# Mamba2 scan and PReLU layer: the order of the third and fourth weight piece, w_out's scales and the rows' scan

## The chip, the cores and the metric

One core of one Trainium2 chip runs the whole program. The time is in microseconds of the device, the median of the runs; less is better. In what follows PE is TensorE (matmuls), DVE is VectorE, ACT is ScalarE, POOL is GpSimd and SP is SyncE, which here only issues DMAs. Each engine works through its own list of instructions in order and waits at an instruction whose inputs aren't there.

## The reference

Two stages in a row: a scan over the sequence in chunks with decays (4 sequences, 8 heads, 768 steps, head size 32, state size 16), and a layer with PReLU on its 3072 x 256 result.

```python
log_a = np.log(np.clip(a, 1e-06, 1.0))
for c in range(nc):
    cum = np.cumsum(la, axis=-1)
    L = np.exp(cum[:, :, :, None] - cum[:, :, None, :]) * causal
    CB = np.einsum('bhin,bhjn->bhij', Cc, Bc)
    y_intra = np.einsum('bhij,bhjd->bhid', CB * L, xc)
    y_inter = np.einsum('bhin,bhnd->bhid', Cc, state) * np.exp(cum)[:, :, :, None]
    y[:, :, sl] = y_intra + y_inter
    state = decay_full[:, :, None, None] * state + np.sum(Bx, axis=2)

x = y.transpose(0, 2, 1, 3).reshape(3072, 256)
h = x @ w_in                                    # 256 -> 2048
g = np.maximum(h, 0.0) + alpha * np.minimum(h, 0.0)
out = g @ w_out                                 # 2048 -> 256
```

The inputs x, a, B, C and alpha are float32; w_in and w_out arrive as float64.

## The kernel before

**Tiling.** The kernel takes chunks of 128 steps, two chunks to a pair, so 12 pairs (pair 0 to 11). Four chunks make a group of 512 tokens. The hidden width of 2048 is cut into 16 blocks f of 128. Group 0 goes block by block: hidden(0, f) is one block's product with w_in and its PReLU (ACT scales by s_alpha, DVE takes the maximum with s_mul times the product), and output(f) the product with w_out, four blocks behind. The groups after it go four blocks at a time (quad and product), with fewer products from sums of the operands. The order on every engine is the order of the program's text, written by hand (manual_schedule).

**The start.** first_two runs pairs 0 and 1, before any group is whole, and mixes their work with the first weights. For pair 1, on PE: the product of B and C (gram_of), one half of hidden_two(0, 2, 0), then x_products (L942) and state_products (L954). times (L900, DVE) makes the operands of x_products; mask (L929, POOL) those of state_products, four of them, of which the fourth is first read by pair 2. copy_out (L962 and L963, four copies on ACT) takes the result out of PSUM into xT; only then can PE multiply the second half of the tokens: hidden_two(0, 0, 2Q, bank(3)), and after first_two, from L1471 on, hidden_two(0, 2, 2Q). hidden_two returns prelu_of[...]: called with False it issues the scaling on ACT alone (L1149), called without it the DVE part (L1154) too, and the scaling where that hasn't been issued.

**Weight pieces.** Both weights are loaded in pieces of 512 KB of float64 (load_next, load_weights, L274), which SP issues, into six buffers "raw". The list pieces holds w_in's first two pieces, and then w_in and w_out by turns: piece 2, the third, is w_in for blocks f = 4 and 5, and piece 3 w_out's first, for f = 0 and 1. A piece is made into float32 from its 32-bit halves in six steps:

- ACT: the absolute of the high half, into wt (L290)
- POOL: a clamp of wt, in place (L295)
- DVE: the sign bit of the high half, into wr (sign, L318)
- DVE: a shift of wt and its xor with wr, into wr (convert_b, L330)
- ACT: the low half, into wg (low; L301 for w_in, for w_out L304 twice, with scales g_mul and g_add by block)
- POOL: wr + wg as whole numbers, into the weight (convert, called by convert_next, L352)

convert_a issues the first two and low; with later=True it returns low, for the caller to issue. g_mul and g_add come from slope_signs (L415): s_mul, of 128 x 16, times 2^-11 and times 2^25.

**Loads of pair 2.** load_pair(2, False, True) issues C in four DMAs (L150), B of its first chunk (L218) and x of its first chunk (L223). The second chunk follows as load_bc2() and load_x(1). rows_sent stores what DVE's scan rows_products (L457) made; pieces 4 to 7 and the decays' rows come behind. All of it is in SP's queue, in this order.

**The rows' scan.** rows_scan(0) (a memset, L481, and a scan, L483, on DVE) makes decays of all rows. PE transposes them (rows_turn, L519) in front of hidden(0, 4), ACT copies that (L524), and POOL's L546 multiplies pair 2's B with them.

**After first_two**: L1471 to L1480 (hidden_two, piece 3's convert_next, rows_turn, piece 4's convert_a and convert_next, the loads of pair 2), and then the loop over f from 4: hidden(0, f), a stage of pair 2 (its first instructions on PE are the transposes L684), then output(f - 4) (L1168), which for f = 4 and 5 reads piece 3.

Of the kernel before, what the change touches and what calls it, by code (L numbers as in the profile page):

```python
# [12 lines left out]
ALU = mybir.AluOpType  # L13
ACTF = mybir.ActivationFunctionType
# [8 lines left out]
def kernel(  # L23
# [25 lines left out]
    nc = tc.nc  # L49
# [46 lines left out]
    gp = ctx.enter_context(tc.tile_pool(name="gp", bufs=16))  # L96
# [6 lines left out]
    def bank(i):  # L103


        return ps_q.tile([P, 512], F32, name="bank", tag=f"q{i}")
# [15 lines left out]
    def load_rows(i, eng=nc.sync):  # L122

        rows = ld.tile([RW, Q], F32, name="rows")
        eng.dma_start(out=rows, in_=a.rearrange("b h (c t) -> (b h c) t", t=Q)[i * RW : (i + 1) * RW])
        loads["r", i] = rows
# [5 lines left out]
    def load_heads(i, eng=nc.sync):  # L132

        eng.dma_start(out=heads_a[i].rearrange("(h n) t -> h n t", n=N)[:, 0],
                          in_=a[0, :, 2 * i * Q : 2 * (i + 1) * Q])
# [26 lines left out]
    def load_tokens(dst, src, t0):  # L162


        d = dst.rearrange("p j (h w) -> p j h w", h=H)
        for k in range(2):
            for j in range(2):
                t = t0 + k * Q + j * HQ
                nc.sync.dma_start(out=d[HQ * k : HQ * (k + 1), j],
                                  in_=src[:, t : t + HQ, :].rearrange("h p w -> p h w"))  # L170
# [16 lines left out]
    def load_products(gp, ap):  # L187
        b, c = divmod(2 * gp, CPB)
        rows = scratch["pf", b // 2].rearrange("(b h c) t -> b h (c t)", b=2, h=H)
        rows = rows[b % 2, :, c * Q : (c + 2) * Q]  # L190
        nc.sync.dma_start(out=ap, in_=rows.unsqueeze(1).to_broadcast([H, N, 2 * Q]))

    def load_pair(gp, decays=True, parted=False):


        b, c = divmod(2 * gp, CPB)
        turned = gp > GC
        nat = ldx.tile([P, 3, 2, H * N], F32, name="nat")
        xt = ldx.tile([P, 2, HD], F32, name="xt")

        ap = ldx.tile([P, 2 * Q], F32, name="ap") if gp >= NB else None
        if gp == 0:
            load_rows(0, nc.scalar)
            load_heads(0, nc.scalar)
        elif gp > NB:
            load_products(gp, ap)
        abc = []
        if gp >= HALF:
            load_tokens(nat[:, 0], B[b], c * Q)
        def load_bc(k):  # L210
            ts = slice((c + k) * Q, (c + k + 1) * Q)
            eng = nc.scalar if gp == 0 else nc.sync
            if gp == 0 and k == 0:
                load_groups(nat, 1, C, b, c)
            if gp in (1, 2) and k == 0:
                load_groups(nat, 1, C, b, c)
            for i, src in enumerate((B,) if turned or gp <= NB else (B, C)):
                eng.dma_start(out=nat[:, i, k].rearrange("p (h n) -> p h n", h=H),  # L218
                              in_=src[b, :, ts, :].rearrange("h p n -> p h n"))

        def load_x(k):
            ts = slice((c + k) * Q, (c + k + 1) * Q)
            nc.sync.dma_start(out=xt[:, k].rearrange("p (h d) -> p h d", h=H),  # L223
                              in_=x[b, :, ts, :].rearrange("h p d -> p h d"))

        for k in range((1 if parted else 2) if gp < HALF else 0):
            load_bc(k)
            if gp >= NB:
                load_x(k)
        for k in range(2 if gp < NB and gp else 0):  # L230
            load_x(k)
        for i, src in enumerate((B, C) if turned else ()):
            load_blocks(nat, i, src, b, c)
        for k in range(2 if gp >= NB else 0):
            abc.append(lda.tile([P, H * Q], F32, name="abc"))
        loads["p", gp] = nat, abc, xt, ap
        if gp >= HALF:
            load_tokens(xt, x[b], c * Q)
        if decays:
            for part in load_spread(gp, b, c):  # L240
                pass
        return lambda: load_bc(1), load_x
# [36 lines left out]
    def convert_a(dst, src, sg, by=nc.gpsimd, later=False):  # L279

        if src.dtype == F32:
            return lambda: None
        raw = raws.pop(id(dst))
        hi = raw[:, :, :, 1]
        half = raw.rearrange("p k w t -> p k (w t)").bitcast(U16)
        half = half.rearrange("p k (w t) -> p k w t", t=4)[:, :, :, 1]
        t = wtp.tile([P, 2, WQ], U32, name="wt")
        g = wtp.tile([P, 2, WQ], F32, name="wg")

        nc.scalar.activation(out=t.bitcast(F32), in_=hi.bitcast(F32), func=ACTF.Abs, scale=0.125)  # L290

        parts[id(dst)] = hi, t, g
        if by is nc.vector:
            sign(dst, src, sg)
        by.tensor_scalar(out=t.bitcast(F32), in0=t.bitcast(F32), scalar1=F64_INF,  # L295
                         scalar2=F64_ZERO, op0=ALU.min, op1=ALU.max)


        def low():
            if sg is None:  # L300
                nc.scalar.activation(out=g, in_=half, func=ACTF.Copy, scale=2.0**-11, bias=2.0**25)  # L301
            for i in range(2 if sg is not None else 0):
                f = slice(sg + i, sg + i + 1)
                nc.scalar.activation(out=g[:, i], in_=half[:, i], func=ACTF.Identity,  # L304
                                     scale=g_mul[:, f], bias=g_add[:, f])

        if later:
            return low
        low()
# [61 lines left out]
    for v in range(2):  # L371
        vs = slice(HQ * v, HQ * (v + 1))
        nc.vector.tensor_copy(out=ident_q[vs].rearrange("p (c t) -> p c t", c=4),
                              in_=ident[vs, vs].unsqueeze(1).to_broadcast([HQ, 4, HQ]))
# [21 lines left out]
    s_mul = const.tile([P, NF], F32, name="s_mul")  # L396
# [12 lines left out]
    def slope_signs():  # L409
        if moe_w_out.dtype == F32:  # L410
            nc.vector.tensor_single_scalar(out=s_out, in_=s_mul.bitcast(U32), scalar=SIGN,
                                           op=ALU.bitwise_and)
        else:
            for o, by in ((g_mul, 2.0**-11), (g_add, 2.0**25)):
                nc.gpsimd.tensor_scalar(out=o, in0=s_mul, scalar1=by, scalar2=None, op0=ALU.mult)  # L415


    xts = {}
# [5 lines left out]
    held = {}  # L424
# [36 lines left out]
    def rows_sent(rpf):  # L461
        scratch["pf", 0] = dr.tile([RW, Q], F32, name="pf0")
        nc.sync.dma_start(out=scratch["pf", 0], in_=rpf)
# [14 lines left out]
    def rows_scan(i):  # L478

        d0 = held[i]  # L480
        nc.vector.memset(d0[:, Q : Q + 1], 0.0)  # L481
        pr = prep.tile([RW, Q], F32, name="pr")
        nc.vector.tensor_tensor_scan(out=pr[:, ::-1], data0=d0[:, 1 : Q + 1][:, ::-1],  # L483
                                     data1=ends[:RW, ::-1], initial=0.0,
                                     op0=ALU.mult, op1=ALU.add)
        return pr
# [350 lines left out]
    def first_two():  # L837
# [141 lines left out]
        def one_at_a_time(i, cs):  # L979
            for c in cs:  # L980
                mask(i, slice(c, c + 1))
# [16 lines left out]
                       in_=ident[:RW, : H * CPB].rearrange("p (h c) -> p c h", c=CPB)[:, :4]  # L998
# [23 lines left out]
        low = convert_a(*pieces[0], later=True)  # L1022
# [13 lines left out]
        low = convert_a(*pieces[1], later=True)  # L1036
# [23 lines left out]
        prelu_of = {0: hidden_two(0, 0, 0, first)}  # L1060
# [12 lines left out]
        hidden_two(0, 2, 0, second, (0,))  # L1073
        states(1, dps, pf1, range(3))
        one_at_a_time(1, range(3))
        slope_signs()
        prelu_of[0](False)
        for r in range(4):
            times(1, r, sp[r])
        states(1, dps, pf1, (3,))  # L1080
        mask(1, slice(3, 4))
        rpf = rows_products()
        load_next()
        load_bc2, load_x = load_pair(2, False, True)
        rows_sent(rpf)
        load_next()
        load_bc2()
# [10 lines left out]
        copy_out(1, y)  # L1098
        prelu_of[2] = hidden_two(0, 2, 0, second, (1,))
        prelu_of[0]()  # L1100
        convert_a(*pieces[2])
        sign(*pieces[2])
        prelu_of[2](False)
        convert_b(*pieces[2])
        convert_next(first=False)
        low = convert_a(*pieces[3], later=True)
        prelu_of[1] = hidden_two(0, 0, 2 * Q, bank(3))
        low()
        prelu_of[2]()
        held["pr"] = rows_scan(0)  # L1110
        convert_b(*pieces[3])
        prelu_of[1]()
        state[0] = new[1][:, 3]
# [325 lines left out]
    pieces = in_pieces[:2]  # L1439
# [4 lines left out]
    def load_next(n=1):  # L1444
        for p in pieces[loaded[0] : loaded[0] + n]:
            load_weights(*p)
        loaded[0] += n

    def convert_next(first=True, ready=False, **kw):


        i = done[0]
        if i < len(pieces):
            if not ready:
                convert(*pieces[i], **kw)
            if first and i and i + 2 < len(pieces):
                convert_a(*pieces[i + 2])
            if loaded[0] == i + 6:
                load_next()
        done[0] += 1  # L1460
# [151 lines left out]
```

## Time and profile before

| What | Value |
|---|---|
| median of 3 runs | 357.13 us (356.59 to 357.65) |
| profiled execution | 356.75 us |
| its span, first to last instruction | 355.0 us |
| clock granted to PE | 1.00 throughout |
| data moved by DMA | 29.82 MB |
| DMA share, 22.4 to 40.6 us | 1.00 |

How it is read: the profile tells of one execution on the chip. Busy is time in which an engine executed; PEld is PE's weight loads, which overlap its matmuls. A wait is idle time in front of an instruction, put down to what ended it; "issue" is idle time that nothing in the profile ended. The chain of waits is followed back from the last instruction, at each step to what released it. The DMA share is the mean busy share of 16 DMA engines, and may be over 100% in short windows, since transfers overlap. On a queue's line in the DMA view stand its name, its packets, its MB and its share of the engines' time in the window.

The start in a few rows of the timelines before (us from the span's start):

| Start | Took | Engine | What |
|---|---|---|---|
| 13.15 | 0.67 | SP | issue of piece 2 |
| 14.37 | 0.43 | SP | issue of piece 3 |
| 14.85 | 1.95 | SP | issue of C of pair 2, four DMAs |
| 16.84 | 0.43 | SP | issue of B of pair 2's first chunk |
| 18.27 | 0.84 | ACT | prelu_of[0](False), L1149 twice |
| 20.02 | 0.58 | POOL | g_mul, L415 |
| 20.57 | 0.25 | POOL | g_add, L415 |
| 20.79 | 0.45 | POOL | fourth mask of pair 1, L929 |
| 21.85 | 0.27 | ACT | first copy of pair 1, L962 |
| 22.55 | 0.69 | ACT | piece 2's L290 |
| 28.30 | 0.38 | PE | transposes of pair 2, L684 |

### The profile page before, as it was taken

To read this page: it belongs to the slowest core of one execution; us is meant where nothing else is said; L and a number is where in the kernel's file an instruction comes from. 1 tells how busy PE (TensorE), PEld (TensorE's weight loads), DVE (VectorE), ACT (ScalarE), POOL (GpSimd) and SP (SyncE) were. 2 spreads that over 40 slices of the span, in tenths; PEclk is the share of its full clock that TensorE was granted. 3 is DMA by queue.
4 is the path that set the end of the run, shared out by engine and by line. 5 is a ranking of instruction groups with operands and counts; after the bars stand their busy time and mean duration, and the time that the engine had idled before them with its cause. 6 is when DMAs were issued, how large, how long until landed. Compare 5 with 4: busy or idle time off the path is not lost.

```text
span 355.0 us, 7785 instructions
## 1 busy us (share of the span) xinstructions
PE 347.8 (98%) x2983; PEld 284.2 (80%) x2983; DVE 237.4 (67%) x482; ACT 172.6 (49%) x391; POOL 205.8 (58%) x230
## 2 busy tenths in 40 slices
PE   8989999999999999999999999999999999999996
PEld 4665665678788788888888888888888888888885
DVE  7968986998758756857747847757856633643363
ACT  4468475526256346346345445345445344443431
POOL 7866668589839755725645725647526535434510
PEclk9999999999999999999999999999999999999999
DMA  6889999117245403403413423422001001001102
GB/s 127 211 172 357 240 313 198 59 30 171 92 88 118 98 3 79 101 2 83 81 48 76 83 52 75 83 53 68 9 2 31 0 2 30 2 1 33 30 0 59
DMA packets 99813, 29.82 MB, mean 84 GB/s; under 512 B 73824, under 2 KB 95680, under 8 KB 99776
## 3 DMA queue, kind: packets, MB, share of 16 engines
q1 hardware_dynamic: 97296, 29.00, 34.8%
q10 hardware_dynamic: 2480, 0.32, 0.6%
q8 instruction: 23, 0.38, 0.4%
q14 instruction: 14, 0.11, 0.1%
HBM read 25.94 MB, written 3.37 MB: 83 GB/s over the span
## 4 chain that ended last, share of the span: by engine, by line
PE 92%; DVE 2%; SPq 2%; POOL 1%; DMA 1%; issue 1%; ACT 0%; POOLq 0%; DVEq 0%
PE bank L1242 33%; PE hp L1267 29%; PE bank L1168 8%; PE ss L1267 6%; PE hp L1125 5%; PE ss L803 1%; PE ss L747 1%; PE bank L1235 1%; PE ss L821 1%; PE ss L795 1%; DMA nat<-in_C_dram 1%; PE ss L758 1%; SPq L1466 1%; DVE dec L884 1%; DVE wr L330 1%
## 5 line engine op out<-in xcount | busy, mean ns | idle before, releaser
L1324 POOL TENSOR_TENSOR gt<-gt 128x512 f32<-128x512 f32 x58 | 74.1, 1278 | 21.1 <-DVE gt L1252 16.3
L1242 PE MATMUL bank<-gt,w_out 128*128 128x256 f32 x320 | 83.5, 381 | 0.0
L1242 PEld LDWEIGHTS bank<-gt,w_out 128*128 128x128 f32 x320 | 60.1, 190 | 9.2 <-issue 1.0
L1314 POOL TENSOR_TENSOR gt<-gt 128x512 f32<-128x512 f32 x20 | 25.4, 1270 | 62.6 <-DVE gt L1252 49.0
L1252 DVE SCALAR_TENSOR_TENSOR gt<-hp,s_mul,gt 128x256 f32<-128x256 f32 x96 | 42.0, 479 | 29.1 <-ACT gt L1250 26.9
L1250 ACT ACTIVATE gt<-hp,s_alpha 128x256 f32<-128x256 f32 x96 | 40.3, 472 | 34.5 <-PE hp L1267 31.4
L1242 PE MATMUL bank<-gt,ws 128*128 128x256 f32 x224 | 55.9, 379 | 0.0
L1242 PEld LDWEIGHTS bank<-gt,ws 128*128 128x128 f32 x224 | 42.3, 190 | 5.6
L1267 PE MATMUL hp<-xs,w_in 128*128 128x256 f32 x160 | 41.9, 384 | 0.0
L1267 PE MATMUL hp<-xs,ws 128*128 128x256 f32 x160 | 41.1, 380 | 0.0
L1293 DVE TENSOR_TENSOR hp<-hp,u 128x512 f32<-128x512 f32 x20 | 14.0, 700 | 35.2 <-ACT u L1291 35.2
L1267 PEld LDWEIGHTS hp<-xs,ws 128*128 128x128 f32 x160 | 30.3, 190 | 4.3 <-POOL xs L1209 0.2
L1267 PEld LDWEIGHTS hp<-xs,w_in 128*128 128x128 f32 x160 | 29.7, 190 | 4.5
L1168 PE MATMUL bank<-w_out,gt 128*128 128x256 f32 x128 | 31.2, 386 | 0.7 <-POOL w_out L352 0.7
L1168 PEld LDWEIGHTS bank<-w_out,gt 128*128 128x128 f32 x128 | 23.6, 190 | 7.6 <-issue 3.1
L1267 PE MATMUL ss<-xT,w_in 128*128 128x256 f32 x96 | 24.6, 379 | 0.0
L659 POOL TENSOR_TENSOR sm<-state,bmask 128x256 f32<-128x256 f32 (+1 forms) x10 | 6.2, 618 | 28.9 <-DVE state L656 28.9
L1125 PE MATMUL hp<-xT,w_in 128*128 128x512 f32 x48 | 22.7, 595 | 0.0
L575 DVE TENSOR_TENSOR_SCAN dec<-abc,bank 128x192 f32<-128x192 f32 x48 | 22.7, 522 | 0.0
L1282 ACT COPY m<-hp 128x512 f32<-128x512 f32 x8 | 4.7, 587 | 35.7 <-PE hp L1267 35.7
L1291 ACT COPY u<-hp 128x512 f32<-128x512 f32 x20 | 11.7, 586 | 19.4 <-PE hp L1267 19.4
L1252 DVE SCALAR_TENSOR_TENSOR gt<-c,s_mul,gt 128x256 f32<-128x256 f32 x40 | 20.6, 554 | 0.0
(231 smaller groups left out, 610.4 us busy)
## 6 DMA issues: line engine op xcount, KB each, us to landing
abc<-z SPq DMA_DIRECT2D x24, 192.0 KB
raw<-in_moe_w_in_dram SPq DMA_DIRECT2D x8, 512.0 KB
raw<-in_moe_w_out_dram SPq DMA_DIRECT2D x8, 512.0 KB
abc<-z SPq DMA_DIRECT2D x8, 512.0 KB
out_dram<-o_sb SPq DMA_DIRECT2D x32, 64.0 KB
xt<-in_x_dram SPq DMA_DIRECT2D x12, 128.0 KB
nat<-in_B_dram SPq DMA_DIRECT2D x24, 64.0 KB
xt<-in_x_dram SPq DMA_DIRECT2D x24, 64.0 KB
```

What stands on the lines that cost most here:

```text
L575: nc.vector.tensor_tensor_scan(out=dv[:, o : o + SQ], data0=abc[k][:, s : s + SQ], data1=ident_p[0][:, :SQ], initial=0.0, op0=ALU.mult, op ...
L659: nc.gpsimd.tensor_tensor(out=sm[:, :nk].rearrange("p k (g m) -> p k g m", g=2), in0=new[:, :nk].unsqueeze(2).to_broadcast([P, nk, 2, 2 * D]),
L1125: nc.tensor.matmul(hp, w_in[:, k, f * P : (f + 1) * P], xts[g][:, k], start=(k == 0), stop=(k == KC - 1))
L1168: nc.tensor.matmul(pos[0][t // 2][:, t % 2], gt[:, t * Q : (t + 1) * Q], w_out[:, f], start=(f == 0 and t % 2 == 0), stop=(f == NF - 1), s ...
L1242: nc.tensor.matmul(ms[g][i][:, h], w, blocks[g, z][n][:, p], start=(q == 0 and h == 0), stop=(q == NQ - 1), skip_group_check=True)
L1250: nc.scalar.mul(o[:, p], h[:, p], s_alpha[:, fs[p]])
L1252: nc.vector.scalar_tensor_tensor(out=o[:, p], in0=h[:, p], scalar=s_mul[:, fs[p]], in1=o[:, p], op0=ALU.mult, op1=ALU.max)
L1267: nc.tensor.matmul(to[:, p], w(2 * z + p), b, start=start and p == 0, stop=True, skip_group_check=True)
L1291: nc.scalar.copy(out=u2, in_=A)
L1293: nc.vector.tensor_tensor(out=Y, in0=Y, in1=u2, op=ALU.add)
L1314: nc.gpsimd.tensor_tensor(out=tc_, in0=g22, in1=g12, op=ALU.subtract)
L1324: eng.tensor_tensor(out=o, in0=x0, in1=x1, op=ALU.subtract)
```

## The change

Four edits, all but one in first_two:

- Piece 2's L290 and L295 are issued right behind prelu_of[0](False) and slope_signs, ahead of times, of pair 1's fourth mask and of its copies; its low stays behind prelu_of[0](). prelu_of[0](False) now stands before slope_signs. prelu_of[2](False) moves behind piece 2's convert_b and convert_next.
- slope_signs makes g_mul and g_add on ACT instead of POOL.
- rows_scan(0) is issued before prelu_of[2](False), and so before the DVE part of prelu_of[2] and piece 3's sign and xor; before, it stood behind prelu_of[2]().
- load_pair gets an argument between, called after each load_bc in its loop. With load_next there, piece 3 is issued behind C and B of pair 2's first chunk, and before its x, instead of ahead of them all.

```diff
-    def load_pair(gp, decays=True, parted=False):
+    def load_pair(gp, decays=True, parted=False, between=None):
...
         for k in range((1 if parted else 2) if gp < HALF else 0):
             load_bc(k)
+            if between is not None:
+                between()
             if gp >= NB:
                 load_x(k)
...
             for o, by in ((g_mul, 2.0**-11), (g_add, 2.0**25)):
-                nc.gpsimd.tensor_scalar(out=o, in0=s_mul, scalar1=by, scalar2=None, op0=ALU.mult)
+                nc.scalar.activation(out=o, in_=s_mul, func=ACTF.Copy, scale=by)
...
         one_at_a_time(1, range(3))
+        prelu_of[0](False)
         slope_signs()
-        prelu_of[0](False)
+        low = convert_a(*pieces[2], later=True)
         for r in range(4):
             times(1, r, sp[r])
         states(1, dps, pf1, (3,))
         mask(1, slice(3, 4))
         rpf = rows_products()
-        load_next()
-        load_bc2, load_x = load_pair(2, False, True)
+        load_bc2, load_x = load_pair(2, False, True, load_next)
         rows_sent(rpf)
...
         prelu_of[2] = hidden_two(0, 2, 0, second, (1,))
         prelu_of[0]()
-        convert_a(*pieces[2])
         sign(*pieces[2])
-        prelu_of[2](False)
+        low()
         convert_b(*pieces[2])
         convert_next(first=False)
+        held["pr"] = rows_scan(0)
+        prelu_of[2](False)
         low = convert_a(*pieces[3], later=True)
         prelu_of[1] = hidden_two(0, 0, 2 * Q, bank(3))
         low()
         prelu_of[2]()
-        held["pr"] = rows_scan(0)
         convert_b(*pieces[3])
```

## The prediction

> **What bounds the kernel now.** First the page: the span and PE's share. PE is busy for 347.8 of 355.0 us, so time can be won only where PE stands still. Then the waits of PE from 17 to 30 us (engine, line, what it waited for: total, times, longest). From 29.3 us to the end that view names one wait, the second one here; the same view from 0 to 29.4 us holds little more than these two and start-up waits of 0.4 us and less.
>
> ```profile
> PE 347.8 (98%) x2983; PEld 284.2 (80%) x2983; DVE 237.4 (67%) x482; ACT 172.6 (49%) x391; POOL 205.8 (58%) x230
> ...
> PE bank L942 <- issue: 1.4, 1, 1.4
> PE bank L1168 <- POOL w_out L352: 0.7, 1, 0.7
> ```
>
> The chain of waits from 17 to 29.5 us tells how the two hang together (start, length, what):
>
> ```profile
> 19.17 1.41 issue
> 20.58 0.42 PE bank L942 x23
> ...
> 22.68 0.57 ACT wt L290
> ...
> 23.32 0.62 POOL wt L295
> ...
> 23.97 0.69 DVE wr L330
> 24.66 0.79 DVE gt L1154 x2
> ...
> 25.49 0.87 DVE pr L483
> 26.36 0.76 DVE wr L318
> ...
> 27.22 0.70 DVE wr L330
> ...
> 28.06 1.28 POOL w_out L352
> ```
>
> The reader sees a serial chain through piece 2 (L290, L295, L330), through DVE's queue (L1154, the rows' scan L483) and through piece 3 (L318, L330, L352) that ends at 29.34, where output(0) on PE starts at 29.39. Its head, L290, stands behind the four copies of pair 1 on ACT, and these behind x_products and state_products, in whose middle PE stood for 1.41 us with no semaphore to wait for. Last, the DMA view over four short windows; in each the line of the data queue and, where there is one, that of the instruction queue q8 (12.7 to 18.3 has none; the others are 18.3 to 19.3 and 40.6 to 41.7 us):
>
> ```profile
> q1 hardware_dynamic: 3597, 1.32, 98.1%
> ...
> q1 hardware_dynamic: 907, 0.24, 105.7%
> q8 instruction: 1, 0.02, 5.8%
> ...
> q1 hardware_dynamic: 594, 0.06, 41.6%
> q8 instruction: 1, 0.02, 5.4%
> ```
>
> The page has 23 packets, 0.38 MB, on q8. PE has 5966 matmuls and loads, so 259 for each packet: q8 carries PE's program in blocks. The first blocks start in windows that open at 10.4, 18.3, 22.4 and 40.6 us, when PE had issued 298, 610, 776 and 928 of them (counts of the windows view). At the mean spacing the second was due at 557, passed before 16 us; it came 2.3 us or more later, after 5.6 us with the data queue at 98%. It is the block beside the 1.41 us, and I take the idle time for a late block of instructions. The fourth also begins only where the load falls from 110% (39.5 to 40.6) to 42%.
>
> **The change, part by part.** The sum goes against the profiled execution's own 355.0 us span (356.75 us in all); the median of the runs, 357.13, is 0.38 above that run, and the gain is taken off the median.
>
> (1) Piece 2's first steps ahead of pair 1's copies. Added to ACT's queue behind L1149 (18.27, two, 0.84, so to 19.11): one L290 of 0.69. Moved forward with it: POOL's clamp L295 (0.61), now ahead of the fourth mask L929 (0.45), which no instruction of PE before pair 2 reads. Cover: ACT idles 2.74 us in front of the copies at 21.85, so it ends by 20.1 with 1.7 us to spare; without that cover the copies and the path would be 0.69 late. Queued behind it are those copies, and PE's bank(3) product behind them; they suffer only if piece 2 isn't there, but the sign step L318 read it at 20.08 without a wait. On POOL: masks to 20.06, clamp to 20.7, mask to 21.2. On DVE: sign 20.08 to 20.5 or 20.9 (0.41 alone, 0.83 beside POOL), L330 to 21.65 instead of 24.66.
>
> (2) w_out's scales by ACT: POOL loses 0.58 and 0.25 us (its two L415), ACT gains two operations on 128x16. No such row on ACT: below, the alpha copy of that shape at 0.18; above, the 128x96 copy at 0.28 (L524). I take the alpha copy's 0.2: 0.4 in all (0.36 to 0.56), in the same 2.74 us of idle time. Without that cover the copies would be 0.4 late.
>
> (3) The rows' scan (memset 0.06, L483 0.87) moves ahead of L1154 into DVE's idle stretch (20.5 to 23.97): 21.7 to 22.6, off the chain. Its reader, the transpose L519, starts only as PE gets there.
>
> (4) Out of the chain are now L290 and the wait for L330, and from DVE's queue 0.93 of scan. Piece 3 then goes, with PE where it is today: L1149 from 23.1, L290 at 23.8, bank(3)'s L1149 when PE's matmuls end (24.83) to 25.7, L304 (1.16) to 26.8, L352 (1.27) to 28.1 instead of 29.34; DVE is done by 26.0 (L1154 from 23.6, L318 0.83, L330 0.69). PE reaches output(0) after the transposes L684: 28.30 plus 0.29 (half of 0.58, which the chain has for four at 50.36) = 28.59. So the wait closes with 0.5 us in hand: 29.39 - 28.59 = **0.80 us**.
>
> (5) Piece 3's load behind C and B of pair 2. SP issues the same DMAs in another order: C from 14.37 (before 14.85), B at 16.35, piece 3 at 16.85 instead of 14.37. C and B gain 0.5 us that nobody needs: their readers start at 28.30 (L684) and 30.93 (the transpose of C). Behind them x waits until 18.02 for an earlier weight transfer in both orders, so from there SP's queue is unchanged (rows_sent 19.42, piece 4 20.43). Piece 3 lands later: the nearest rows are piece 1 (issued 7.74, its L290 released by it at 11.48: 3.7 us) and piece 2 (issued 13.15, read without a wait at 20.08: at most 6.9). So 20.6 to 23.8; its first reader, L290, is due at 23.8 with PE as today and at 22.5 at the earliest. I take 20.6, as today's queue has run dry by then (30% share from 20.6 to 21.6). At the other end it would be 1.3 late and, with 0.5 in hand, cost 0.8.
>
> What it brings is the gap it leaves in the data: piece 2 (0.52 MB at the 302 GB/s of 15 to 16.5 us) is drained by about 17, and landed at 18.02, when it releases x on SP; then come only C and B (4 x 32 KB + 64 KB) until piece 3, issued 16.85, arrives about 1.1 us later (piece 4: issued 20.43, load up at 21.6). If the block of instructions gets in there, it starts near 17 instead of 18.3 or later and is ready 1.3 us or more earlier. That is the one unknown price. From below nothing (the block comes as before) or a loss (second rival); from above the whole 1.41, since the masks on POOL end at 20.06: L954's last pair could run at 20.1 and, at 0.32 each, be out at 20.45, when the copies can start instead of 21.85. I take **1.4**, because blocks one and four begin as a run of load ends.
>
> With that, everything of (4) moves too: copies to 21.3, piece 2's L352 to 23.2, PE at hidden(0, 4) at 25.15, L304 to 25.3, piece 3's L352 to 26.7, PE at output(0) at 27.2. Sum: 0.80 + 1.41 = 2.2 us. Past 29.4 PE never waits, so the shift is kept if the others keep up: POOL's L352 of pieces 4 and 5 end at 32.74 and 36.0 for products at 35.11 and 36.82, and start from chains that move as much.
>
> By the Trainium skill (Runtime: NRT & Kernel Launch, Instruction fetch mechanics) programs come in 16 KiB blocks, which the 23 packets bear out, but PE holds 2048 instructions and refills are mostly hidden; here PE stood after some 690. By DMA: Bandwidth & Descriptors (Queues, rings and completion order) an engine turns from queue to queue after each packet, so no block waits out a load. By either rule (5) is worth nothing and the sum is 0.80: 356.3.
>
> **Forecast:** 357.13 - 2.2 = **354.9 us**; with a block that still holds PE for up to 0.7, and the spread of the runs (0.5 either way), 354.1 to 355.7. Chance 0.48.
>
> **Rivals.** *The block comes as late as before* (or the 1.41 has another cause at a fixed place of PE's program): only 0.80 is won, 356.3 (355.9 to 356.6). For it: the profile calls the gap "issue", no more. Against: the late spacing. 0.25.
>
> *Slower: the block waits until the whole run is dry.* Place: the same spot in L942. The gap is filled by C and B, the block stands behind piece 3 and x, and starts near 20.9 (today's drain) instead of 18.3: ready 2.6 later, at 23.2. Less the 0.80, output(0) starts 1.8 late: 358.9. It decides once the block starts over 1.9 us (0.80 + 1.07) later than today. Against: in before it started while the load was at 106%. 0.16.
>
> *The gain is partly taken back*: DVE is at 95% from 36 to 50 us (13.33 of 14), and output(4) at 45.04 starts as POOL's L352 ends. If 1.5 of the 2.2 goes there, 356.4 (355.6 to 357.0); against it, DVE's stretch starts from work that is early as well. 0.11.
>
> **Chances.** A measurement here can't tell less than 0.3% (1.07 us) from no change. Faster: the forecast's 0.48, plus 0.06 of the first and 0.04 of the last rival, 0.58; slower: 0.16, and 0.02 of the last rival; the rest, 0.24, is same. The range, 354.1 to 357.0, leaves out the slower rival and 0.04 at its ends.
>
> **What would show it.** PE's L942 without idle time, or with 1.41; q8's second packet before 18 us; L290 of piece 2 at about 19.5 and not later than the copies; no PE wait at L1168; L483 before 23. A copy L962 that waits for L290, or an L290 of piece 3 that waits for its load, would make the prediction wrong.

## The result and the profile after

| | before | after |
|---|---|---|
| median of 6 runs | 356.86 us (356.26 to 357.65) | 354.76 us (354.26 to 355.06) |
| profiled execution | 356.75 us | 354.47 us |
| its span | 355.0 us | 352.8 us |
| clock granted to PE | 1.00 | 0.999 |

The ratio of after to before is 0.994, with a 95% interval of 0.9924 to 0.9956. The forecast was 354.9 us, in a range of 354.1 to 357.0. Behind load_pair, the lines of after are those of before plus 2 (L942 is now L944, L1168 is L1170); in the kernels of the experiments they can stand one off.

The page of after, the row of busy time and the row of the chain that ended last:

```profile
PE 348.2 (99%) x2983; PEld 285.2 (81%) x2983; DVE 238.3 (68%) x482; ACT 172.8 (49%) x393; POOL 204.8 (58%) x228
...
PE 94%; SPq 3%; DMA 1%; POOL 1%; issue 0%; DVE 0%; POOLq 0%
```

PE's work is as long as before (348.2 against 347.8 us), and the span is 2.2 us shorter: the whole difference is idle time. POOL has two instructions fewer, ACT two more. The waits of PE from 0 to 29.4 us (total, times, longest):

```profile
PE hp L362 <- PEq L1598: 0.8, 1, 0.8
PE ss L910 <- DMA xt<-in_x_dram: 0.4, 1, 0.4
```

Both belong to the start. The first is in before too, at L360 with 0.8 us; the prediction, which speaks of start-up waits of 0.4 us and less, left it out. The two rows that the forecast was about, "issue" at x_products and POOL's w_out at output(0), are gone, and from 29.3 us to the end the view names none. The chain from 19 to 29 us, which in before went through ACT, POOL and DVE, is PE alone:

```profile
19.33 0.56 PE bank L944 x33
...
20.96 1.06 PE hp L1142 x4
22.02 1.73 PE bank L1142 x8
...
25.56 1.75 PE hp L1127 x4
27.31 0.22 PE ss L686 x2
27.53 1.73 PE bank L1170 x8
```

What feeds it, in ACT's and POOL's timelines of after (start, length, instruction, and in brackets the idle time before it and what ended that):

```profile
18.73 0.84 ACT L1151 ACTIVATE gt<-hp,s_alpha 128x256 f32<-128x256 f32 x2 [2.23 <-POOL s_alpha L409]
19.45 0.21 ACT L417 ACTIVATE g_mul<-s_mul 128x16 f32<-128x16 f32 x1
19.56 0.21 ACT L417 ACTIVATE g_add<-s_mul 128x16 f32<-128x16 f32 x1
19.67 0.66 ACT L292 ACTIVATE wt<-raw 128x512 f32<-128x512 f32 x1
20.73 0.27 ACT L964 COPY xT<-ss 128x128 f32<-128x128 f32 x1 [0.41 <-PE bank L956]
...
25.73 1.28 POOL L354 TENSOR_TENSOR w_out<-wr,wg 128x512 uint32<-128x512 uint32 x1 [0.94 <-ACT wg L306]
```

Piece 2's L292 now stands ahead of the copies, and the copies still wait for PE, so it delays nothing. Piece 3 is in w_out at 27.01, and PE starts output(0) at 27.36: 0.35 us of room. The DMA view of after from 16.5 to 18.3 us:

```profile
q1 hardware_dynamic: 1010, 0.50, 93.9%
q8 instruction: 1, 0.02, 3.2%
```

In before, q8 had no packet in that window. The second packet of PE's program starts at 17.05 us by the trace and has ended at 17.97; in before it ran from 18.35 to 19.27.

### The profile page after: what moved, and what is told of

The parts are those of the page before. It is cut to its first block, busy times and chain, and to the rows that moved or that the text cites. A ratio compares the mean times of both kernels' runs of the same rounds, so it can differ in the third digit from the quotient of the medians.

```text
span 352.8 us, 7784 instructions
## 1 busy us (share of the span) xinstructions
PE 348.2 (99%) x2983; PEld 285.2 (81%) x2983; DVE 238.3 (68%) x482; ACT 172.8 (49%) x393; POOL 204.8 (58%) x228
## 4 chain that ended last, share of the span: by engine, by line
PE 94%; SPq 3%; DMA 1%; POOL 1%; issue 0%; DVE 0%; POOLq 0%
PE bank L1244 34%; PE hp L1269 29%; PE bank L1170 8%; PE hp L1127 6%; PE ss L1269 6%; PE ss L805 1%; PE ss L749 1%; PE hp L1142 1%; DMA xt<-in_x_dram 1%; PE bank L1237 1%; PE ss L823 1%; PE ss L797 1%; SPq L223 1%; PE ss L760 1%; SPq L1468 1%; PE ss L634 1%
## 5 line engine op out<-in xcount | busy, mean ns | idle before, releaser
L1170 PE MATMUL bank<-w_out,gt 128*128 128x256 f32 x128 | 31.1, 384 | 0.0
L1170 PEld LDWEIGHTS bank<-w_out,gt 128*128 128x128 f32 x128 | 23.6, 190 | 6.5 <-issue 3.1
L1303 DVE TENSOR_TENSOR c<-hp,m 128x512 f32<-128x512 f32 x20 | 13.8, 691 | 10.0 <-PE hp L1269 9.9
```

The costliest lines, as they stand in the source:

```text
L1170: nc.tensor.matmul(pos[0][t // 2][:, t % 2], gt[:, t * Q : (t + 1) * Q], w_out[:, f], start=(f == 0 and t % 2 == 0), stop=(f == NF - 1), s ...
L1303: nc.vector.tensor_tensor(out=c22, in0=A, in1=m5, op=ALU.add)
```

## The experiments

Each kernel is compared with before, run on the same chip in the same batch. A change of 0.3% is near what a median of a dozen executions can tell, so the profile of each is read as well.

**The load order alone.** Before, with the last of the four edits only:

```diff
-        load_next()
-        load_bc2, load_x = load_pair(2, False, True)
+        load_bc2, load_x = load_pair(2, False, True, load_next)
```

> The kernel before with nothing but piece 3's load behind C and B of pair 2. Theory: the second block of PE's program (q8) starts near 17 us instead of 18.3, PE's 1.4 us of idle time inside x_products is gone, pair 1's copies start near 20.5, and the wait of 0.7 us at output(0) stays, since piece 2's and piece 3's steps are in the old order: 1.4 us less than before, 355.4. Rival (the 1.4 us has its cause at a fixed place of PE's program, the order of loads doesn't touch it): no change, 356.9, PE idle 1.4 us as before.

355.64 us (355.35 to 356.1, 12 executions) against 356.68 of before (35): ratio 0.997 (0.9953 to 0.9988); span 353.9. PE's waits from 17 to 29.4 us in its profile:

```profile
PE bank L1169 <- POOL w_out L354: 0.7, 1, 0.7
```

The stop in x_products is gone and the wait at output(0) stays, so the two are separate prices, as the forecast had them. The block started at 13.92 us in this execution, ahead of 14.17, where SP begins the first DMA that stands in another order. So in this one execution the load order can't have brought it early; that the order counts is read from the twelve executions and from the next two kernels.

**Everything but the load order.** After, with that line put back as in before.

> The changed kernel with piece 3's load back ahead of C and B. Theory: block two starts at 18.3 or later, PE stands some 1.4 us in x_products, no wait at output(0): 1.4 us more than the changed kernel, 0.8 less than before, 356.1. Rival: no idle time in x_products, 354.8 as with the whole change.

355.71 us (355.18 to 359.31, 12 executions); ratio 0.9998 (0.9972 to 1.0025). The median is 0.97 below before's, while the ratio is spoilt by four executions from 356.70 to 359.31. The profile is of the longest. Its waits of PE from 17 to 29.4 us:

```profile
PE bank L944 <- issue: 1.9, 1, 1.9
```

The windows behind it (start and end, length, busy time and instructions of PE, PEld, DVE, ACT and POOL, granted clock, DMA share, GB/s):

```profile
20.00:21.50 1.50, 0.25 (x20) 0.25 (x23) 1.40 (x3) 0.00 (x0) 0.98 (x2) 0.83 0.40 57
21.50:27.00 5.50, 5.50 (x47) 4.58 (x32) 0.83 (x4) 2.60 (x8) 1.26 (x1) 0.50 0.71 159
27.00:28.00 1.00, 1.00 (x5) 0.79 (x4) 1.00 (x3) 0.23 (x1) 0.61 (x1) 0.58 0.95 322
```

The stop is back, 1.9 us of it. There is no wait at output(0), but with PE this late its absence says little about the other three edits; the eight executions at full clock, with a median of 355.66, say more. What no step had foreseen is the clock in the last columns: from 21.00 us, shortly before the stop ends at 21.25, it is 0.50, for 6.83 us by the trace's clock records, and the eight matmuls of L1143 that take 1.89 us elsewhere take 3.00. By this reading it is the lowered clock that makes 359.31 of an execution that would else lie near 355.7.

**The gap filled.** After, with piece 4's load (as large as piece 3's, 512 KB) where piece 3's had been. The computation is the same.

```diff
+        load_weights(*pieces[4])
         load_bc2, load_x = load_pair(2, False, True, load_next)
         rows_sent(rpf)
-        load_next()
+        loaded[0] += 1
```

> The changed kernel, with piece 4's load (512 KB, the size of piece 3's) issued in the place that piece 3's load left, so that data runs on there; ACT's, POOL's and DVE's lists are the changed kernel's. Theory (the block comes late because it waits while a run of weight data goes on): block two starts at 18.3 us or later again and PE stands 1 to 1.6 us in x_products: about 356.1. Rival (what counted was piece 3 itself, or C and B being early): block near 17, no idle time, 354.8.

355.69 us (354.59 to 359.22, 12 executions); ratio 0.9979 (0.995 to 1.0008). PE's waits from 17 to 29.4 us:

```profile
PE bank L944 <- issue: 2.0, 1, 2.0
```

Its DMA view from 18.2 to 20 us:

```profile
q1 hardware_dynamic: 1080, 0.39, 97.6%
q8 instruction: 1, 0.02, 4.1%
```

With other data in the place, the block is late again (18.24 us) and the stop is back in the profile; in one of the twelve executions, at 354.59, it can hardly have been. So it isn't piece 3's content or its lateness that helps, but that no 512 KB are queued ahead of C and B. The block also didn't wait for the queue to run dry: it started with q1 at 97.6% over this window, so the slower rival of the forecast has the wrong picture of what holds it.

**Where the stop stands.** Before, with 24 more instructions of PE early in the program (12 loads and 12 matmuls, whose result nobody reads):

```diff
-    keep_warm(first, 2, GT)
+    keep_warm(first, 8, Q)
```

> The kernel before with its first warm-up of PE cut finer: 8 matmuls of 128 columns instead of 2 of 512, the same time on PE, but 24 more instructions (12 matmuls, 12 weight loads) ahead of everything. Theory (PE stands at the border of a block of its program): it stands after the same count from the start, 690 matmuls and loads, so x_products has some 29 matmuls ahead of the idle time instead of 41; the time stays within 0.5 us of before. Rival (a fixed place in the program, by a wait of that instruction): still 41 matmuls of x_products ahead of it.

356.73 us (355.58 to 357.14, 10 executions); ratio 1.0002 (0.9983 to 1.0021). Two windows, up to the stop and in it:

```profile
0.00:18.70 18.70, 17.71 (x345) 13.44 (x345) 16.23 (x44) 9.12 (x22) 15.98 (x36) 1.00 0.77 181
18.70:20.00 1.30, 0.00 (x0) 0.00 (x0) 1.30 (x5) 0.23 (x1) 1.30 (x4) 1.00 0.18 33
```

PE stops after the same count, 345 matmuls and 345 loads, as in before. Of x_products, 93 matmuls are recorded up to there (pair 0's included), in before 105. The stop has moved 12 matmuls up in the computation and stays where it was in the instruction stream. It is a border of the program's blocks, not something in x_products.

The four profiles and those of before and after give one more row: when the block's packet ended, and when PE, if it stood, went on (from the trace).

| Kernel | packet | PE stood | went on |
|---|---|---|---|
| before | 18.35 to 19.27 | 1.41 | 20.58 |
| all but the load order | 18.82 to 19.92 | 1.9 | 21.25 |
| gap filled | 18.24 to 19.43 | 2.0 | 20.93 |
| 24 instructions more | 16.49 to 18.76 | 1.4 | 20.12 |
| after, profiled again (below) | 17.44 to 18.38 | 0.5 | 19.90 |
| after | 17.05 to 17.97 | 0 | |

PE goes on 1.31 to 1.52 us after the packet has ended, in all five. What the load order separates is the packet's end, more than its start. In the four profiles with 512 KB queued ahead of C and B it ended at 18.76 to 19.92 us, and PE stood in each; with 24 more instructions it started early, at 16.49, and took 2.27 us. In the ten profiles with piece 3 behind them (all other kernels here) it ended at 15.32 to 18.38, and PE stood for it in one, 0.5 us.

**The other three edits, one undone at a time.** After, with the scan back behind prelu_of[2]():

```diff
-        held["pr"] = rows_scan(0)
         prelu_of[2](False)
...
         prelu_of[2]()
+        held["pr"] = rows_scan(0)
```

> After, with the rows' scan back behind the DVE part of prelu_of[2]. In the profile of after, DVE's L332 of piece 3 ends at 25.52 and POOL's L354 of piece 3 starts only at 25.73, held by ACT's L306, and ends 0.36 us before PE reaches output(0) at 27.36. Theory (the three moves share 0.36 us of room, now that the load order has removed the stop): the scan goes from 22.5 to about 23.8 and pushes piece 3's sign and xor by 0.4 to 0.5 us; POOL's L354 starts 0.2 later, output(0) waits for at most 0.1 us: 354.8, within 0.3 us of after. Rival (each of the moves is needed): piece 3 is late by the scan's 0.93 less 0.36, a wait of PE at output(0) of 0.57 us for POOL's w_out: 355.3.

355.49 us (354.11 to 355.76, 12 executions); ratio 0.9933 (0.9905 to 0.9961). No wait at output(0) in the profile, and the lower group of its executions, 354.11 to 354.66, lies where after's do (the upper one is taken up below). The move isn't needed once the others are there (undoing it together with the scales wasn't run). The same for the scales, made by POOL again (nc.gpsimd.tensor_scalar in slope_signs):

> After, with g_mul and g_add made by POOL again (0.58 and 0.25 us there in before), ahead of piece 2's clamp. Theory: the clamp goes from 20.55 to about 21.3, DVE's xor of piece 2 from 21.73 to about 22.1, piece 2's L354 ends 0.3 later, piece 3's clamp and xor 0.3 later, and as ACT's L306 is what releases piece 3's L354, output(0) doesn't wait: 354.8. Rival: POOL's 0.83 us come through whole, less the 0.36 of room: a wait of 0.47 us, 355.2.

354.90 us (354.29 to 355.65, 12 executions); ratio 0.9925 (0.9894 to 0.9955); no wait of PE from 17 to 30 us. Last, piece 2's first steps back behind the copies:

```diff
-        low = convert_a(*pieces[2], later=True)
...
+        convert_a(*pieces[2])
         sign(*pieces[2])
-        low()
```

> After, with piece 2's L292 and clamp back behind pair 1's copies. Theory: on ACT the copies end at 21.6 as in after, L292 and L303 follow to 22.9, everything of piece 3 on ACT comes 0.6 to 0.7 us later, and with 0.36 us of room PE waits at output(0) for 0.2 to 0.35 us for POOL's w_out: 355.0. It is the move that counts most of the three. Rival (the move is worth nothing once the load order is changed): no wait at output(0), 354.8. Other rival (the chain through piece 2 is what the forecast said, with nothing in hand): a wait of 0.7 us, 355.5.

355.97 us (354.86 to 356.61, 12 executions); ratio 0.9957 (0.9931 to 0.9984). PE's wait at output(0):

```profile
PE bank L1169 <- POOL w_out L354: 0.6, 1, 0.6
```

The chain in front of it:

```profile
22.48 0.17 ACT xT L965
22.65 0.58 ACT wt L292
...
23.30 0.63 POOL wt L297
...
23.95 0.69 DVE wr L332
...
24.80 1.40 POOL w_in L354
...
26.28 0.68 POOL wt L297
...
26.99 0.70 DVE wr L332
...
27.83 1.29 POOL w_out L354
```

Of the three, this one carries the gain: with the copies ahead of piece 2's L292 the chain of before is back, without the scan, and PE waits 0.6 us for it. My 0.2 to 0.35 was too low: the chain runs on POOL here, where piece 3's clamp stands behind piece 2's L354, and I had let ACT decide.

**What lowers the clock.** After, with work on DVE that nobody reads, so that PE stands at the same place for a semaphore instead of for instructions:

```diff
+        nc.vector.memset(idle, 0.0)
+        for r in range(3):
+            nc.vector.scalar_tensor_tensor(out=idle, in0=idle, scalar=2.0, in1=idle,
+                                           op0=ALU.mult, op1=ALU.max)
         for r in range(4):
             times(1, r, sp[r])
```

> After, with a memset and three operations of 128 x 512 added on DVE in front of pair 1's times, whose results nobody reads: PE has to stand for about 1.5 to 2 us in front of x_products, in the place of before's stop but by a semaphore, not for instructions. What is asked is the granted clock. Theory (standing still for 1.4 to 2 us at this place is what is followed in some executions by the clock at 0.50, whatever the cause): of some 12 executions several lie 1 to 3.5 us above the fastest, with a mean granted clock of 0.990 to 0.996, as before's do (355.2 to 359.9); median 356.5 to 358. Rival (it is the late block of instructions, or something beside it): every execution has a clock of 0.999 or 1.000, all lie within 1 us of each other, at 356.3 to 356.8.

359.85 us (358.86 to 361.68, 12 executions); ratio 1.0074 (1.0048 to 1.01). PE's one wait from 17 to 30 us:

```profile
PE ss L945 <- DVE dec L903: 2.5, 1, 2.5
```

The window behind it, with the columns as above (the granted clock is the third from the end):

```profile
23.60:27.00 3.40, 3.40 (x10) 2.77 (x9) 1.73 (x6) 2.58 (x8) 1.26 (x1) 0.51 0.73 184
```

All 12 executions have a mean clock of 0.990 to 0.995. The median is 5.0 us above after's 354.84 (14 executions), and in the profile only 2.5 of it is the stop itself. The block's packet had ended at 18.07 here, and PE went on at 21.20. So no late block is needed for the clock to fall: standing still near this place is enough. With one of the three operations in place of three:

> After, with the memset and one of the three operations on DVE that stopped PE for 2.5 us, so that PE stands for 0.6 to 1.0 us in front of x_products. Theory (a stop has to fill enough of some stretch of time in which PE's activity is counted): no execution shows a clock below 0.998, and the price is the stop alone, 0.6 to 1.0 us over after of the same runs: 355.4 to 356.2. Rival (any stop at this place can bring the clock down): 2 or more of 12 executions have a clock of 0.995 or less and lie 1 to 3.5 us higher.

356.52 us (355.02 to 358.89, 12 executions); ratio 0.998 (0.9955 to 1.0006). Two executions (357.04 and 358.89) have a clock of 0.995, so my theory that a short stop is safe fell. But the profiled execution shows only 0.2 us of stop, PE being late by itself (it stood 0.6 us for POOL's w_in at 18.84), and how long PE stood in those two isn't known. From which length on the clock falls stays open.

**Two groups of executions.** After once more, unaltered:

> The changed kernel once more, unaltered, beside the next two, since the kernels with one move undone showed executions in two groups about 1 us apart (with the scan back: 354.1 to 354.7 and 355.4 to 355.8). Theory (the groups come from the start, where B or x of pair 1 lands up to 1 us later in some executions, and belong to no edit): after shows them too, 354.2 to 354.9 and 355.2 to 355.7, median 354.7 to 355.4, every clock at 0.998 or higher. Rival (they come from the undone moves): one group, 354.2 to 355.1.

355.19 us (354.49 to 356.66, 8 executions); ratio 0.9952 (0.9936 to 0.9968). Four lie at 354.49 to 354.90, three at 355.48 to 355.66, one at 356.66. The groups belong to no edit of the last experiments. In the profiled execution, one of the lower group (354.90), PE's waits from 17 to 29.4 us had one row:

```profile
PE bank L944 <- issue: 0.5, 1, 0.5
```

The margin that the load order gives the block is thus used up in some executions.

A guess at the cause, alpha's load, which takes SP 2.41 us to issue, moved to ACT's queue:

> After, with the load of alpha (8 KB, 16 rows) issued by ACT behind the copy into prt instead of by SP, where its issue took 2.41 us at 5.26 in the profile of after. Theory (SP's issues set the start: the chain of after runs through them from 3.4 to 12.9 us, and PE waits 0.38 us for x of pair 1): the loads of piece 1 and pair 1 are issued about 0.45 us earlier, the wait goes: 354.4, median below after's of the same runs by 0.3 to 0.4. Rival (the 2.41 us are a wait for an earlier transfer, which then stands in front of piece 1): no more than 0.1 us. From the other side: with everything 0.45 us earlier, the instruction block again meets a run of data, PE stands 1.4 us or more: 355.8 to 356.2.

354.95 us (353.83 to 355.98, 6 executions); ratio 0.9941 (0.992 to 0.9962). The issue of piece 1, next in SP's queue, now took 2.56 us: the wait belongs to the place in the queue and not to alpha. The two groups stayed.

The traces with one edit undone show what the upper group is. POOL's timeline with the scan back:

```profile
5.54 0.65 POOL L455 TENSOR_SCALAR rz<-rows 96x127 f32<-96x127 f32 x1
8.24 0.70 POOL L548 TENSOR_TENSOR bn<-nat,prt 128x256 f32<-128x256 f32 x1 [2.05 <-DMA nat<-in_B_dram]
8.88 0.10 POOL L556 MEMSET gt<- 128x4 f32 x1
9.07 1.06 POOL L455 TENSOR_SCALAR gt<-a 128x252 f32<-128x252 f32 x1
```

In after's profile L548 started at 6.68. Pair 0's B lands later in some executions, POOL stands for it, and its clamp of a (L455), which doesn't need B, comes behind. The profiles bear this out: with the scan back, with piece 2's first steps back and with alpha on ACT, all three of an upper group, L548 starts at 8.24 to 8.36, and PE later stands 0.57 to 0.58 us for POOL's w_in, near 18.8; in after, in after once more and with the scales on POOL, all of a lower group, L548 starts at 6.49 to 6.84 and that wait isn't there. So the last experiment turns the two round:

```diff
-        bn0 = pair_loads(0)
         z1 = first_a(heads_a[1], nc.gpsimd, lent[1][:, 2:])
+        bn0 = pair_loads(0)
```

> After, with pair 0's clamp of a (POOL, L455, 1.06 to 1.23 us) ahead of pair 0's product of B (POOL, L548) instead of behind it. Where pair 0's B lands late (in the profile with the scan back, POOL stands 2.05 us for it, until 8.24, and everything behind comes 1.0 us later to PE's pair 1), the clamp now runs while POOL waits. Theory (the upper group of executions is this wait): L548 ends by 8.9 in either case, ahead of its reader L910 on PE at 9.26 and of POOL's L976 at 9.12; the upper group falls from 355.5 to at most 355.0, all executions lie within 354.0 to 355.2, the median at 354.5, a ratio to before of 0.993 to 0.994. Rival (B's late landing holds PE and ACT as well, by 0.3 to 0.65 us, and that is what comes through): two groups stay, the upper 0.3 to 0.6 above the lower, median 354.9. From the other side: the clamp is late for the early executions, which lose 0.3 to 0.5: 355.1 and over.

354.37 us (353.98 to 354.74, 6 executions) against 356.76 of before; ratio 0.9928 (0.9908 to 0.9948). One group, no wait of PE from 17 us on, span 352.5. It is the fastest median here, 0.4 below after's first six runs and 0.8 below its second eight; but the intervals of the ratios overlap, and six executions don't prove that the upper group is gone.

## Why the prediction was right

**The sum.** The forecast took 2.2 us off 357.13. Before's six runs have a median of 356.86, and 2.10 was won, so a lower start and a smaller gain both had a part in 354.76. In its second batch the change won 1.54 us (355.19 against 356.73). From the profile of before to that of after, output(0) starts 2.03 us earlier (29.39 to 27.36), the span ends 2.2 us earlier. By place: pair 1's half of hidden_two on PE starts 0.46 us later in after (17.82 against 17.36), which no edit explains; from there to state_products (20.93 against 19.82) 1.57 us are won, where step (5) said 1.41; from the transposes L684 (28.30 against 27.14) to output(0) 0.87 us, where step (4) said 0.80; another 0.05 lies between. Step (5) and step (4) were each a little low, and the start took some of it back. In medians the load order alone is worth 1.04 and the three others 0.97 us, the change 2.10 on its own first runs (0.88 and 0.87 for the two parts if only executions at full clock are taken): they about add up, though the split is nearer to half and half than the forecast's 1.41 and 0.80.

**(1)** Right. L292 ran at 19.67 (19.5 expected) with the copies behind it still waiting 0.41 us for PE. On POOL and DVE piece 2 was later than worked out, its xor ended at 22.49 (21.65 expected), of which 0.46 is the later start. It is also the edit that makes step (4): without it, a wait of 0.6.

**(2)** Right. The two scales took 0.21 us each, against 0.2 from the alpha copy, inside ACT's idle time. Their move away from POOL is worth nothing that shows (354.90 without it).

**(3)** Right about the chain, L485 ran at 22.54. Step (4) counts its 0.93 among what leaves the chain, but that share isn't needed: with the scan back in its place output(0) doesn't wait.

**(4)** Right. Piece 3 was in w_out at 27.01 (26.7 expected) and PE was there at 27.36 (27.2): room of 0.35 us for an expected 0.5. What held piece 3's L354 at the end was ACT's L306, as the working had it.

**(5)** Right in its result; of its reason one half is shown. Shown is that the stop is a late block: it stands at a border of the instruction stream (24 more instructions leave the count at 345 and 345), and PE goes on 1.31 to 1.52 us after the packet's end. Shown too is that a load of 512 KB queued ahead makes the packet end late and brings the stop back. The block started at 17.05, in the 17 that was expected. Not shown is the gap that was to let it in. Three windows of after (columns as above, the DMA share is the last but one):

```profile
16.00:17.00 1.00, 0.62 (x38) 0.37 (x38) 1.00 (x2) 0.45 (x2) 1.00 (x2) 1.00 1.02 381
17.00:17.70 0.70, 0.70 (x34) 0.60 (x32) 0.60 (x3) 0.00 (x0) 0.70 (x1) 1.00 1.08 342
17.70:18.10 0.40, 0.40 (x5) 0.28 (x2) 0.36 (x3) 0.00 (x0) 0.32 (x2) 1.00 0.67 141
```

The packet started with the load at its full height, which falls only when the packet is nearly over. In the kernel with the gap filled, too, it started in a window at 97.6%. How a load queued ahead delays the packet stays open.

That the whole 1.41 was won owes something to luck. In after PE came to the border 0.53 us later than in before (the first matmul behind it started at 19.47, 1.49 us after the packet's end), since pair 1's half of hidden_two had started 0.46 late. At before's pace it would have run out of work at 19.17, and by the 1.31 to 1.52 it would have stood an estimated 0.1 to 0.3 us. In the profile of after once more it stood 0.5, within the 0.7 that the forecast allowed for.

The rival that the block comes as late as before fell with the profile of after: the stop is gone and the packet started at 17.05. Its price was about right: the kernel without the load order, which has just this, wins 0.97 us by its median, where the rival had 0.80. The rival with the loss given back to DVE fell too: behind 29.3 us PE waits for nothing.

The Trainium skill (Runtime: NRT & Kernel Launch, Instruction fetch mechanics) has the fetch mostly hidden, and DMA: Bandwidth & Descriptors (Queues, rings and completion order) has an engine turn from queue to queue after each packet. Both would have made step (5) worth nothing. Here PE stood 1.4 to 2.0 us for a block in four kernels, and behind a data load the packet ended 0.8 to 1.9 us later than in after. When PE's block was asked for, no trace shows. The measurement decides, whichever of the two rules is the one that doesn't fit.

**What it missed** is the clock. Of 100 executions of before, run beside the experiments, 25 had a mean clock of 0.996 or less, and lay at 356.76 us and above, up to 360.83 (one at 367.61), where before's median is 356.73. Of 14 of after, none had, and none of the 60 of the six other kernels that have its load order and no work added on DVE. In the three kernels with 512 KB queued ahead 11 of 34 had. So the change takes away a tail as well, which before's profiled execution, at 1.00, couldn't show. The medians move by little for it: before's is 356.67 without those 25.

## What to carry to other kernels

An idle stretch that ends without a semaphore can be a late block of the program: count the instructions up to it, move the count, and see whether it stays. The order of the loads in front of it is then a lever, even where the data have time to spare. And where one short wait on the main engine has a spread of some us behind it, look at the clock of each execution before you look for the spread elsewhere.

## What the runs showed of the hardware

- With a stop of PE of 1.9, 2.0 and 2.5 us in the profile the granted clock fell to 0.50, for 6.83, 6.83 and 3.4 us. With a stop of 1.4 us it fell in the profile of the kernel with 24 more instructions, for 3.41 us, and in before's not at all. Of the executions of these two, 3 of 10 and 25 of 100 had a lowered clock; how long PE stood in them isn't known but for the profiled ones.
- The place of the fall isn't set by the stop alone. By the clock records of these four traces it fell 17.06 or 17.07 us after it had risen to 1.00 (3.94 to 21.00, 4.35 to 21.42, 6.58 to 23.64, 5.14 to 22.21), which is five times 3.41, and so 1.7 to 4.9 us after the stop had begun.
- The Trainium skill (TensorE: Matmul & The Clock Gate, What's actually happening) says that an idle window of about 3.4 us halves the clock, that the window runs freely, and (Why this matters for your kernels) that gaps of PE should stay under about 3 us. The lengths here, 3.4 and 6.83 us, are one and two such windows, and both the steps of 3.41 and that the clock of one kernel falls in some executions alone agree with a window that runs freely. That the gap must be 3 us long doesn't hold here: 1.9 us did it, and in one profile 1.4, with the small matmuls of x_products (64 x 32) around it. Whether those count as half idle wasn't tried.
- PE goes on 1.31 to 1.52 us after its block's packet has ended, so by estimate its packet has to start 2.2 to 2.4 us ahead of the block's first instruction (with 0.92 us of transfer, as in before and after; in one kernel it took 2.27).
